# Folding the column frequencies of an inverse transform over plus and minus f, in a fused spectral and MLP block on one Trainium2 core

## The chip, the core and the metric

The kernel runs on one core of a Trainium2 chip. The metric is the device time of one execution in microseconds (us); the figure of a kernel is the median of its runs. For the kernel before the change, three runs gave 366.99, 367.8 and 368.43 us.

## The reference

Only what matters is kept: a layer norm with modulation, a two-dimensional spectral filter, a gated residual, and a Mish MLP with its own norm and gate. Sequence length is 2048, width 512, hidden width 1376, all float32.

```python
mod = (silu(c) @ w_mod).reshape(1, 6, 1, 512)
sa, ca, ga, sb, cb, gb = (mod[:, k] for k in range(6))
h = layernorm(x) * (1 + ca) + sa
x = x + ga * irfft2(rfft2(h) * (w_r + 1j * w_i), (2048, 512))
h = layernorm(x) * (1 + cb) + sb
x = x + gb * (mish(h @ w1 + b1) @ w2)
```

## The kernel before

The work has four stages, one behind the other, and TensorE runs through all of them. Every transform is a product with a constant matrix. A product of two float32 operands takes two passes over TensorE (so the trace counts two MATMUL records for it); the large MLP products are instead split by hand into a high and a low part in the type fp32r, and three one-pass products (`TERMS`) make one.

**Stage one** takes the 16 slices n of 128 rows through the row transform (`p1_row`, L269) and the first half of the column transform (`p1_col`, L314 to L316).

**Stage two** (`p2_*`, L441 to L698) handles the 64 row frequencies q in 17 groups, mostly of four. For each q TensorE turns a 128x128 block (`p2_in`, L539); one product with the matrix `kf` for the whole group ends the forward transform (`p2_mul`, L559); ScalarE (ACT), GpSimd (POOL) and VectorE (DVE) multiply by the complex filter (`p2_prod`, L590 to L593) and add the two products (`p2_add`, L599) into `slot(g)`, which lies in `a_sb`; then for each q one product of 128 column frequencies by 128 with the matrix `kv` starts the way back (`p2_out`, L608). `store_d` copies the result into `dd`, where it stands on 128 partitions, one for each column frequency, with three planes: real, imaginary, and minus real. The third plane is written by ACT (L454), DVE (L456) or POOL (L458). The group of q = 0 has its own path (`z_in` to `z_out`, with the helper `reflected`). The seven `mod_late` sums of modulation columns (L176 on DVE) are placed between the groups.

**Stage three** ends the column transform. For each n and each of four j, `p3_col` forms one sum of two products: real and imaginary planes times `kc[0]` (L859), imaginary and minus real planes times `kc[1]` (L860). ACT copies the result out of PSUM (`buf`, L862), `p3_row` does the row transform with the gated matrix `kiv` (L869), DVE adds to x (L872), and ACT takes the sums for the second norm (`row_squares`, L876 and L877). Beside it ACT and DVE split the weights w1 into high and low parts (L739, L740), form the sums of blocks of w1 (L760) and of w2 (`sum_w2`, L913, into `tsum`) that Strassen's scheme needs, split those too (L916, L917, L926, L1339), and bring the first rows of the normed x into the layout of the MLP (`norm_one`, L219; `turn_near`, L798; a round trip through memory; `scale_turned`, L825; `split_in`, L850 and L851).

**Stage four** is the MLP on eight blocks b of 256 rows, taken in four pairs i. The up products use Strassen's seven products (`up`, L991) but for the first pair, which is plain (`PLAIN`, L974). After Mish, `sums` (L1061) forms four block sums, `halves` splits the blocks (L916, L917), and `down` (L1091) does seven products for each hidden tile t, with three terms of 256 columns each: 21 passes. `gather`, `chain` and `residual` (L1114 to L1143) put the seven results together, multiply by the gate, and POOL's queue adds the block to x by a DMA.

Stages one and two are written out by hand in program order. Stages three and four are recorded as steps in a `Plan`, and the table of numbers `ORDER` sets the order in which the steps are issued. Within an engine the issued order is the executed order.

## Time and profile before

| What | Value |
|---|---|
| Median of the three runs | 367.8 us |
| Profiled execution, its own time | 368.36 us |
| Its span, first to last instruction | 366.6 us |
| Granted TensorE clock | 0.997 |
| TensorE busy in the span | 358.6 us (98%) |
| DVE busy | 302.5 us (83%) |
| ACT busy | 266.9 us (73%) |
| POOL busy | 78.3 us (21%) |

The profile shows one execution. "PE" rows are products on TensorE, "PEld" rows the loading of their stationary operand. Busy time of PE overstates its work, since the record of a product runs on while the next one already streams; so the pace of products is read here from start to start, not from the mean of a row. A line number is that of the kernel whose trace it is.

### The profile page before, as it was taken

Reading aid. Unit: us, or ns where it says so; the run is one execution under the profiler, and the core shown is the slowest. Engines: PE = TensorE matmul, PEld = TensorE weight load, DVE = VectorE, ACT = ScalarE, POOL = GpSimd, SP = SyncE. Lnnn points to the kernel's source line nnn. Section 1 sums busy time; section 2 is a strip of 40 time slices with the busy share of each in tenths; the row PEclk is TensorE's granted clock in tenths of the full one; section 3 lists DMA queues with packets and bytes.
Section 4 is the critical chain, followed back from the end, with each engine's and each line's share of the span. In section 5 each row is a group of like instructions: output and inputs, shape, how many; then the busy total and the mean of one; then the engine's idle time right before and its main releaser. Section 6 shows DMA issues by size and latency. Waiting matters only on the chain.

```text
span 366.6 us, 7820 instructions
## 1 busy us (share of the span) xinstructions
PE 358.6 (98%) x2666; PEld 333.9 (91%) x2666; DVE 302.5 (83%) x752; ACT 266.9 (73%) x601; POOL 78.3 (21%) x126
## 2 busy tenths in 40 slices
PE   8999999998999999999999999999999999999994
PEld 8999977777999998798999999999999999999994
DVE  1898968888889799998994777998759977887995
ACT  1798879996799999998773878766577753555650
POOL 0588738786011001100002101004100000000000
PEclk9999999999999999999999999999999999999998
DMA  7999997678498776899888877786989678863133
GB/s 254 383 349 377 331 373 250 219 185 305 142 327 254 236 256 230 278 306 322 248 225 292 276 236 200 207 276 206 281 301 243 215 229 266 227 219 62 59 57 115
DMA packets 54343, 89.96 MB, mean 245 GB/s; under 512 B 7552, under 2 KB 20960, under 8 KB 54048
## 3 DMA queue, kind: packets, MB, share of 16 engines
q1 hardware_dynamic: 49728, 74.65, 62.0%
q0 software_dynamic: 2416, 7.87, 9.0%
q10 hardware_dynamic: 2160, 6.95, 6.0%
q8 instruction: 21, 0.34, 0.4%
q14 instruction: 18, 0.15, 0.1%
HBM read 68.21 MB, written 17.57 MB: 234 GB/s over the span
## 4 chain that ended last, share of the span: by engine, by line
PE 84%; ACT 5%; DVE 4%; DMA 2%; POOL 1%; issue 1%; ACTq 1%; SPq 0%; DVEq 0%; POOLq 0%
PE bank L1091 25%; PE bank L991 22%; PE bank L974 6%; PE bank L269 4%; PE bank L869 4%; PE bank L859 3%; PE bank L860 3%; PE bank L1037 3%; PE bank L314 3%; PE bank L1087 3%; DMA hT<-in_B_w_dram 2%; PE bank L1103 2%; PE bank L316 1%; PE bank L315 1%; PE bank L325 1%
## 5 line engine op out<-in xcount | busy, mean ns | idle before, releaser
L991 PE MATMUL bank<-hT,wr 128*128 128x256 f32 x360 | 51.6, 283 | 0.0
L991 PEld LDWEIGHTS bank<-hT,wr 128*128 128x128 f32 x360 | 47.3, 191 | 0.6
L991 PE MATMUL bank<-hB,wr 128*128 128x256 f32 x318 | 46.6, 285 | 0.0
L991 PEld LDWEIGHTS bank<-hB,wr 128*128 128x128 f32 x318 | 41.9, 191 | 0.9
L1143 POOL DMA_DIRECT2D x<-modr x7 | 6.3, 898 | 140.5 <-DVE modr L1142 84.7
L1091 PE MATMUL bank<-w2a,ah 128*128 128x256 f32 x161 | 35.1, 283 | 0.0
L917 DVE TENSOR_TENSOR al<-buf,ah 128x512 fp32r<-128x512 f32 (+1 forms) x45 | 30.1, 668 | 5.7 <-ACT ah L916 4.7
L1091 PE MATMUL bank<-w2b,ah 128*128 128x256 f32 x147 | 32.2, 283 | 0.0
L916 ACT CAST ah<-buf 128x512 fp32r<-128x512 f32 (+1 forms) x45 | 27.0, 602 | 4.5 <-DVE buf L1061 2.6
L1091 PEld LDWEIGHTS bank<-w2a,ah 128*128 128x128 f32 x161 | 27.0, 191 | 0.4
L859 PE MATMUL bank<-kc,d 128*128 128x128 f32 x128 | 24.9, 276 | 0.5 <-ACT d L452 0.5
L1091 PEld LDWEIGHTS bank<-w2b,ah 128*128 128x128 f32 x147 | 24.9, 191 | 0.3
L860 PE MATMUL bank<-kc,d 128*128 128x128 f32 x128 | 24.8, 275 | 0.0
L974 PE MATMUL bank<-hB,wr 128*128 128x512 f32 x96 | 24.4, 393 | 0.0
L1091 PE MATMUL bank<-w,ah 128*128 128x256 f32 x112 | 21.5, 284 | 0.0
L314 PE MATMUL bank<-buf,mring 128*128 128x512 f32 x48 | 20.6, 430 | 0.2 <-DVE buf L307 0.2
L974 PEld LDWEIGHTS bank<-hB,wr 128*128 128x128 f32 x96 | 17.3, 189 | 3.1
L859 PEld LDWEIGHTS bank<-kc,d 128*128 128x128 f32 x128 | 19.4, 192 | 0.7 <-ACT d L452 0.7
L860 PEld LDWEIGHTS bank<-kc,d 128*128 128x128 f32 x128 | 19.5, 192 | 0.0
L1091 PEld LDWEIGHTS bank<-w,ah 128*128 128x128 f32 x112 | 17.7, 191 | 0.6
L608 PEld LDWEIGHTS bank<-kv,a_sb 128*128 128x128 f32 x126 | 15.5, 192 | 2.8 <-issue 2.2
L788 POOL DMA_DIRECT2D turned<-x x16 | 8.9, 568 | 42.1 <-DVE x L782 42.1
(310 smaller groups left out, 1098.2 us busy)
## 6 DMA issues: line engine op xcount, KB each, us to landing
wr<-w_S SPq DMA_DIRECT2D x60, 256.0 KB, 4.0
wr<-w_A SPq DMA_DIRECT2D x45, 256.0 KB, 3.8
w_S<-hT SPq DMA_DIRECT2D x20, 256.0 KB, 2.9
x<-in_A_x_dram SPq DMA_DIRECT2D x16, 256.0 KB, 4.7
xring<-in_x_t_dram SPq DMA_DIRECT2D x16, 256.0 KB, 4.6
w_A<-wr SPq DMA_DIRECT2D x15, 256.0 KB, 3.1
x<-modr POOLq DMA_DIRECT2D x7, 512.0 KB, 5.5
out_dram<-x SPq DMA_DIRECT2D x7, 512.0 KB, 3.8
```

Source lines behind the costliest of these rows:

```text
L269: nc.tensor.matmul(pgv[:, j], data(j), krs[:, j, :].rearrange("p (c q) -> p c q", c=2), start=True, stop=True)
L314: nc.tensor.matmul(pa, m[:, a, 0:128], g, start=(i == 0), stop=False)
L608: nc.tensor.matmul(pd[:, i * P:(i + 1) * P], y[:, i * P:(i + 1) * P], kv[:, 0:128], start=True, stop=True)
L859: nc.tensor.matmul(o, dj[:, 0:128], kc[0][:, n, :], start=True, stop=False)
L860: nc.tensor.matmul(o, dj[:, 64:192], kc[1][:, n, :], start=False, stop=True)
L869: nc.tensor.matmul(px[:, j * P:(j + 1) * P], e[:, j * P:(j + 1) * P], kiv[:, j, :], start=True, stop=True)
L916: nc.scalar.copy(h, r)
L917: nc.vector.tensor_tensor(l, r, plain(h), op=ALU.subtract)
L974: nc.tensor.matmul(ups[i, t, f], ring[t, a][:, p, b, :], sides[int(a[2]) - 1][:, :, q, b, :], start=(a[2] == "1" and b == 0 and n == 0), s ...
L991: nc.tensor.matmul(o, w[:, p, k, :], h[:, q, k, :], start=(first and n == 0), stop=(last and n == 5), skip_group_check=True)
L1037: nc.tensor.matmul(ups[i, 0][:FL], w1s[:, p, u, :], sides[u // 2][:, :, q, u % 2, :], start=(u == 0 and p + q == 0), stop=(u == 3 and p == ...
L1091: nc.tensor.matmul(out_ps[b][n][:, 256 * half:256 * half + 256], a[p][:, e], w2[t][q][:, r], start=(t == 1 and half == 0 and i == 0), stop ...
```

## The change

1. **Signs and fold.** The 128 column frequencies stand in a new order, 64, -1 to -63, 0 to 63, so that plus and minus f lie 64 columns apart. After the filter two new operations per group (`fold`) replace the two halves by their difference and their sum. The column matrix then needs cosines for one half and sines for the other, and `p3_col` needs one product where it had two. `kc` is half as large, and the third plane of `dd` is gone.
2. **The way back in halves.** The sums and the differences need different matrices (`kv` and i times `kv`), so each product of L608 becomes two, each with 64 columns of the stationary operand, into 64 partitions of the result (`half`). The column of frequency 64, which has no partner, needs a small product of its own for each batch of groups (`spin_mul`), and a copy back (`spin_copy`).
3. **First superblock plain through w2.** `PLAIN_DOWN = 2`: blocks b = 0 and 1 do `down` without Strassen, 12 passes of 512 columns for each t where there were 21 of 256; `sums`, `gather` and `chain` fall away for them, and `halves` splits 512 columns where it split 896.
4. **Sums of w2 later.** They are formed only behind block 1, from w2 loaded once more (`load_sums`, two loads for each t).
5. **Steps on GpSimd.** The first four `norm_one`, the first 16 operations of `scale_turned`, and the scaling in `row_squares` move from ACT to POOL.
6. **Order.** Stage two is recorded as a `Plan` as well, and both stages have new tables (`ORDERS`).

The core of the diff (constants and the q = 0 path are cut):

```diff
+PLAIN_DOWN = 2
-RAW = ((0, 0, 0, 0), (1, 0, 2, 1), (2, 0, 1, 6))
-SUM = ((0, 1, 3, 3), (3, 0, 4, 4), (3, 1, 5, 5), (1, 1, 6, 2))
+RAW = ((0, 0, 0, 0), (1, 0, 2, 1), (2, 0, 1, 5))
+SUM = ((0, 1, 3, 3), (3, 0, 4, 6), (3, 1, 5, 4), (1, 1, 6, 2))
...
-    dd = [big.tile([P, 8, 4, 3, NQ], F32, name=f"d{i}", tag=t) for i, t in enumerate(("da", "db"))]
+    dd = [big.tile([P, 8, 4, 2, NQ], F32, name=f"d{i}", tag=t) for i, t in enumerate(("da", "db"))]
...
-            if kind == "all":
-                nc.scalar.mul(minus, s[:, :, 0, :], -1.0)
-            elif kind != "pool" and i:
-                nc.vector.tensor_scalar(minus, s[:, :, 0, :], -1.0, None, op0=ALU.mult)
-            else:
-                nc.gpsimd.tensor_scalar(minus, dst[:, :, 0, q0:q0 + nq], -1.0, None, op0=ALU.mult)
...
+    def half(out, rows, *products):
+        o = out[rows:rows + 64]
+        for n, (a, b) in enumerate(products):
+            nc.tensor.matmul(o[0:1] if a.shape[1] == 1 else o, a, b, start=(n == 0), stop=(n == len(products) - 1))
...
+    def fold(g, step):
+        less, more = halves_of(g)
+        if step == 0:
+            on = nc.gpsimd if FOLD(g) else nc.vector
+            on.tensor_tensor(less, more, less, op=ALU.subtract)
+        else:
+            nc.vector.scalar_tensor_tensor(more, more, 2.0, less, op0=ALU.mult, op1=ALU.subtract)
...
+    def spin_mul(gs):
+        st["pd", gs[0]] = pd = bank("DA"[gs[0] > 14])
+        y = single(gs)
+        nc.tensor.matmul(pd[:, 0:y.shape[1]], kv[:, 6 * P:7 * P], y, start=True, stop=True)
+
+    def spin_copy(gs):
+        y = single(gs)
+        nc.scalar.copy(y, st["pd", gs[0]][:, 0:y.shape[1]])
...
-            nc.tensor.matmul(pd[:, i * P:(i + 1) * P], y[:, i * P:(i + 1) * P], kv[:, 0:128],
-                             start=True, stop=True)
+            for lo in (0, 64):
+                half(pd[:, i * P:(i + 1) * P], lo, (y[:, i * P + lo:i * P + lo + 64], kv[:, P - 2 * lo:2 * P - 2 * lo]))
...
+    BATCHES = [(1, 2), (3, 4), (5, 6), (7, 8), (9, 10), (11, 12), (13, 14), (15,), (16,)]
...
-        st["h2", n] = norm(n, True)
+        st["h2", n] = norm(n, n > 3)
...
-            nc.scalar.activation(o, o, AF.Identity, bias=cols[:, 1, 0, k:k + 1], scale=cols[:, 1, 1, k:k + 1])
+            if near:
+                nc.gpsimd.tensor_scalar(o, o, cols[:, 1, 1, k:k + 1], cols[:, 1, 0, k:k + 1], op0=ALU.mult, op1=ALU.add)
+            else:
+                nc.scalar.activation(o, o, AF.Identity, bias=cols[:, 1, 0, k:k + 1], scale=cols[:, 1, 1, k:k + 1])
...
-            nc.tensor.matmul(o, dj[:, 0:128], kc[0][:, n, :], start=True, stop=False)
-            nc.tensor.matmul(o, dj[:, 64:192], kc[1][:, n, :], start=False, stop=True)
+            nc.tensor.matmul(o, dj, kc[0][:, n, :], start=True, stop=True)
...
-        nc.scalar.mul(mv[:, n, 0:1], mv[:, n, 0:1], -D ** -1.5)
+        nc.gpsimd.tensor_scalar(mv[:, n, 0:1], mv[:, n, 0:1], -D ** -1.5, None, op0=ALU.mult)
...
+    def load_sums(t):
+        for e, f, rows in tiles(t):
+            nc.sync.dma_start(modr[:rows, e], w2_d[f * P:f * P + rows, :])
...
-        if b == NB - 1 and t > 2:
+        if b < PLAIN_DOWN or b == NB - 1 and t > 2:
             parts[b, t] = [(w, slice(0, 4))]
             return
...
+            if t and b < PLAIN_DOWN:
+                n, half, f = piece
+                w = w2[t][q]
+                w = w[:, 1:3] if f else w[:, 0:4:3]
+                nc.tensor.matmul(out_ps[b][n], a[p][:, half + 2 * f], w, start=(t == 1 and f == 0 and i == 0),
+                                 stop=(t == NT - 1 and f == 1 and i == 2), skip_group_check=True)
...
+    for t in range(1, NT):
+        at = start[PLAIN_DOWN - 1, t] + 3
+        plan.at(at, load_sums, t)
+        plan.at(at + 1, sum_w2, t, 0, 1, 2, 3)
+        plan.at(at + 2, split_w2, t, True)
```

How the order moves at three places. First TensorE at the end of stage two and the start of stage three, before. `kv,a_sb` is the way back, `wide,kf` and `buf,kf` the last forward products, `kc,d` the column products:

```order
L559 MATMUL bank<-wide,kf 128x512
L608 MATMUL bank<-kv,a_sb 128x128 x4
L559 MATMUL bank<-buf,kf 128x512
L608 MATMUL bank<-kv,a_sb 128x128 x20
L859 MATMUL bank<-kc_1088,d_749 128x128
L860 MATMUL bank<-kc_1116,d_749 128x128
```

The same place of the changed kernel, where `a_sb,kv` is `spin_mul` and `64x128` are the halves:

```order
L566 MATMUL bank<-buf,kf 128x512
L480 MATMUL bank<-kv,a_sb 64x128 x16
L633 MATMUL bank<-a_sb,kv 128x4
L633 MATMUL bank<-a_sb,kv 128x8
L480 MATMUL bank<-kv,a_sb 64x128 x24
L633 MATMUL bank<-a_sb,kv 128x4
L480 MATMUL bank<-kv,a_sb 64x128 x8
L974 MATMUL bank<-kc,d_749 128x128 x8
L983 MATMUL bank<-kiv,buf 128x128 x4
```

The way back now comes in batches of two groups, twice as many products of half the height, with small products between; the column products alternate no longer between two matrices.

Second DVE in the middle of stage two, before. L593 is the filter product, L599 the addition, L456 and L450 the third plane and the copy into `dd`:

```order
L599 TENSOR_TENSOR a_sb<-bank,wide 128x512
L593 TENSOR_TENSOR bank<-bank,wqa 128x512
L456 TENSOR_SCALAR d_750<-bank 128x32x4
L599 TENSOR_TENSOR a_sb<-bank,buf 128x512
L593 TENSOR_TENSOR bank<-bank,wqa 128x512
L450 COPY d_750<-bank 128x32x2x4
L456 TENSOR_SCALAR d_750<-bank 128x32x4
```

And of the changed kernel (L622 and L624 are the two steps of `fold`):

```order
L622 TENSOR_TENSOR a_sb<-a_sb 128x4x63
L612 TENSOR_TENSOR a_sb<-bank,buf 128x512
L624 SCALAR_TENSOR_TENSOR a_sb<-a_sb 128x4x63 x2
L622 TENSOR_TENSOR a_sb<-a_sb 128x4x63
L456 COPY d_750<-bank 128x64x4
L608 TENSOR_TENSOR bank<-bank,wqa 128x512
L624 SCALAR_TENSOR_TENSOR a_sb<-a_sb 128x4x63 x2
L612 TENSOR_TENSOR a_sb<-bank,buf 128x512
```

The operation for the third plane is gone, and up to two fold operations per group stand between addition and filter product.

Third ACT at the start of stage three, before (`mv<-mv` is the scaling, `w_1221<-modr` the high part of the sums of w2):

```order
L862 COPY buf<-bank 128x512
L739 CAST hT_1311<-hT_1310 128x256
L739 CAST wr<-hT_1279 128x256
L916 CAST w_1221<-modr 128x1024
L876 ACTIVATE mv<-mv 128x1
L877 ACTIVATE bank,mv<-x,mv 128x512
L188 ACTIVATE rstd<-mv,eps 128x2
```

And of the changed kernel:

```order
L976 COPY buf<-bank 128x512
L196 ACTIVATE rstd<-mv,eps 128x2
L197 ACTIVATE rstd<-rstd 128x2
L991 ACTIVATE bank,mv<-x,mv 128x512
L976 COPY buf<-bank 128x512 x2
L851 CAST hT_1413<-hT_1412 128x256
```

The scaling and the sums of w2 have left the queue, and the splits of w1 come later.

422 lines of the change are left out of this document (241 added, 181 removed), and 97 rows, old and new, of tables (ORDER, ORDERS).

## The prediction

> **What bounds the kernel now.** I read the first part of the page, then the shares of the chain that ended last, then the busy time by stage. A window row gives its bounds, its length, and then busy us and instructions of PE, PEld, DVE, ACT and POOL, the granted clock, and the DMA share and rate.
>
> ```profile
> PE 358.6 (98%) x2666; PEld 333.9 (91%) x2666; DVE 302.5 (83%) x752; ACT 266.9 (73%) x601; POOL 78.3 (21%) x126
> ...
> PE 84%; ACT 5%; DVE 4%; DMA 2%; POOL 1%; issue 1%; ACTq 1%; SPq 0%; DVEq 0%; POOLq 0%
> ```
>
> ```profile
> 49.60:90.00 40.40, 38.86 (x240) 28.42 (x239) 33.92 (x73) 36.33 (x88) 30.15 (x52) 1.00 0.78 265
> 90.00:129.10 39.10, 38.74 (x343) 38.55 (x344) 33.85 (x95) 35.58 (x91) 2.86 (x5) 1.00 0.75 238
> 129.10:146.30 17.20, 17.20 (x122) 15.96 (x121) 16.24 (x46) 16.39 (x43) 1.07 (x2) 1.00 0.73 242
> 146.30:177.30 31.00, 31.00 (x185) 27.21 (x184) 28.73 (x73) 28.67 (x68) 1.09 (x2) 1.00 0.92 301
> 177.30:220.00 42.70, 42.70 (x345) 41.88 (x344) 32.87 (x87) 29.11 (x59) 5.34 (x9) 1.00 0.84 250
> ```
>
> TensorE is the bound in every stage, at full clock: 84% of the chain lies on it. So the change is worth what it takes from TensorE's queue, as long as the others keep up. In stage two (first row) and stage three (the next two) ACT and DVE are at 84% to 95% themselves, so a shorter TensorE queue meets them soon; after 177.3 they have room. POOL has room from 90 on.
>
> The pace of products comes from the timeline, start to start (start, length, engine, line):
>
> ```profile
> 118.52 1.06 PE L869 MATMUL bank<-kiv,buf 128*128 128x128 f32 x8
> 119.41 0.39 PE L859 MATMUL bank<-kc,d 128*128 128x128 f32 x2
> 119.63 0.39 PE L860 MATMUL bank<-kc,d 128*128 128x128 f32 x2
> ```
>
> ```profile
> 65.59 1.02 PE L559 MATMUL bank<-buf,kf 128*128 128x512 f32 x2
> 66.45 0.60 PE L539 MATMUL bank<-ident,a_sb 128*128 128x128 f32 x4
> 66.89 0.39 PE L475 MATMUL bank<-kv,early 128*128 128x128 f32 x2
> 67.20 0.38 PE L476 MATMUL bank<-kv,early 128*1 128x128 f32 x2
> 67.51 0.49 PE L478 MATMUL bank<-kw,early 96*128 96x128 f32 x2
> ```
>
> Four products (eight passes) of L869 take 0.89 us, one of L859 0.22 us: a 128x128 product of two passes costs 0.223 us. A product with `kf` takes 0.86 us, four turns 0.44. L476 uses one column of the stationary operand and streams 128: it takes 0.31 us like the full L475 ahead of it. Each is about 0.09 us over the pace, which I read as the price of a change of shape; without it the one-column product costs as much as a full one.
>
> **The change, part by part.** All is summed against the profiled execution (368.36 us, span 366.6); it lies 0.56 us above the median of 367.8, to which I carry the sum.
>
> *Column products.* These rows give the counts in passes (two for one product):
>
> ```profile
> L859 PE MATMUL bank<-kc,d 128*128 128x128 f32 x128 | 24.9, 276 | 0.5 <-ACT d L452 0.5
> L860 PE MATMUL bank<-kc,d 128*128 128x128 f32 x128 | 24.8, 275 | 0.0
> L608 PE MATMUL bank<-kv,a_sb 128*128 128x128 f32 x126 | 16.7, 278 | 0.9 <-DVE a_sb L599 0.7 <-ACT d L454 0.2
> ```
>
> One of the two lines goes: 64 products at 0.223 us, **-14.3 us** of TensorE. Before, stage three is TensorE's from end to end, so nothing else hides this time.
>
> *The way back in halves.* 63 products of L608 cost 14.0 us; 126 halves replace them. Their price is in no row. From above, a half streams the same 128 columns as L476, so 0.223 us each, 28.1 in all. From below, half the work of a full product, 0.112 us each, 14.0 in all. The one-column row would speak for the upper end, but there a single product stands between two full ones; here the halves alternate between two sets of 64 columns and two sets of 64 result partitions in runs of 14 to 24, and one needs nothing of the other. I take the lower end as the likelier: the two share one product's time, and TensorE's sum stays as it was. The upper end is the first rival.
>
> The Trainium skill, page "TensorEngine Tiling (Array Packing)", section "Tiling Modes", says that tiles of 128x64 work independently and can run in parallel, and that a change of mode drains the engine. By it the halves would cost 14 us and not 28; the 0.09 us around L476 agrees with the drain, and no run here shows two halves side by side.
>
> Added to TensorE are nine small products (at 0.223 us, bound by the one-column row, 2.0 us), about 18 changes of shape around nine runs of halves (at 0.09, 1.6 us), and some 0.4 us in the q = 0 path: +4.0 us. TensorE's work in stage two is now 16 products with `kf` (13.8), 63 turns (6.9), 14.0 and about 2 for q = 0, 36.7 of 40.4 us; it becomes 40.7.
>
> *DVE in stage two.*
>
> ```profile
> L456 DVE TENSOR_SCALAR d<-bank 128x128 f32<-128x128 f32 x9 | 2.6, 284 | 0.5 <-ACT d L452 0.5
> L913 DVE TENSOR_TENSOR modr<-wide 128x256 f32<-128x256 f32 x10 | 4.2, 415 | 0.0
> L176 DVE SCALAR_TENSOR_TENSOR wm<-wm,bank 128x512 f32<-128x512 f32 x7 | 4.7, 679 | 0.0
> ```
>
> The third plane goes (-2.6 us), two of the seven modulation sums move ahead of the stage (-1.4). Of the 32 fold operations 25 stand on DVE, each 252 elements a partition; by the nearest row, 256 elements in 0.415 us, +10.4 us. 33.9 becomes 40.3 us in a stage of 40.4. It was 6.5 us idle, mostly while the first groups fill the pipeline, and it will not work without gaps; the additions behind the folds wait in the same queue, and TensorE waits for those. Bounds: nothing if the folds overlap perfectly, +6.5 if all the old idle time stays. I take **+5.0 us** for the stage, in which TensorE's own +4.0 lies hidden. ACT there loses L454 and gains nine small copies,
>
> ```profile
> L454 ACT ACTIVATE d<-bank 128x128 f32<-128x128 f32 x7 | 2.1, 295 | 0.0
> L521 ACT COPY early<-bank 32x1 f32<-32x1 f32 x1 | 0.1, 150 | 0.0
> ```
>
> about equal. POOL loses 13 planes at 0.53 and gains seven folds,
>
> ```profile
> L458 POOL TENSOR_SCALAR d<-d 128x128 f32<-128x128 f32 x13 | 6.8, 530 | 0.0
> L262 POOL TENSOR_TENSOR mring<-mraw,mring 128x256 fp32r<-128x256 f32 x16 | 12.2, 763 | 13.2 <-ACT mring L261 13.2
> ```
>
> -6.9 and +5.3 in 30.2 us. Neither binds.
>
> *Plain down for two blocks.* From the chain, in runs:
>
> ```profile
> 146.46 6.14 PE bank L974 x27
> 176.84 1.44 PE bank L1091 x12
> ```
>
> 512 columns in fp32r take 0.227 us, 256 take 0.120. Per block and t, 12 x 0.227 = 2.73 against 21 x 0.120 = 2.52; ten of them, **+2.1 us** of TensorE, with nothing to hide it. What it takes from DVE and ACT (four sums, the smaller split, `gather` and `chain`) lies beside TensorE.
>
> *Steps on POOL, later sums.*
>
> ```profile
> L876 ACT ACTIVATE mv<-mv 128x1 f32<-128x1 f32 x16 | 3.2, 200 | 0.0
> L219 ACT ACTIVATE buf<-x,nmr,rstd 128x512 f32<-128x512 f32 x8 | 6.3, 818 | 0.0
> L825 ACT ACTIVATE wide<-wide,cols 128x256 f32<-128x256 f32 x12 | 6.5, 593 | 0.0
> L916 ACT CAST w2a<-modr 128x1024 fp32r<-128x1024 f32 x1 | 1.0, 1042 | 0.0
> L917 DVE TENSOR_TENSOR w2a<-modr,w2a 128x1024 fp32r<-128x1024 f32 x1 | 1.2, 1217 | 0.0
> ```
>
> Between 90 and 129.1 ACT loses about 14 x 0.2, 4 x 0.82, 8 x 0.59 and two casts of sums at 1.04: about 13 of 35.6 us, as much as TensorE loses (14 of 16 slices, 12.5), so its share stays near 85%. DVE loses eight sums at 0.415 and two splits at 1.217, 5.8 of 33.9: 28.1 us remain, where TensorE needs 39.1 - 12.5 = 26.6. So DVE becomes the longer by **+1.5 us**; from 129.1 on it has twelve sums and three splits less and catches up, so this is not paid twice. POOL takes these 36 operations, none over the 0.82 us that ACT needs for the longest if POOL is no slower, where it was busy for 4 of 56 us; at twice ACT's price they are some 32 us and still fit. What is queued behind them is its sends of normed rows, and the split of the first blocks waits for those. The later sums (5 x (4 x 0.415 + 1.22) = 14.4 us of DVE) fall where 177.3 to 220 shows DVE at 77%, and blocks 0 and 1 give back about as much. Ten more loads of 256 KB there, 2.6 MB beside 10.7 MB (42.7 us at 250 GB/s), feed sums that block 2 is the first to need, so other blocks' products hide them; if a load came late, its transfer of about 1 us at that rate and the sum and split behind it would stand open, some 4 us once. One load of `kc` falls away.
>
> Sum: -14.3 + 5.0 + 2.1 + 1.5 = **-5.7 us**, so 362.7 by the profiled execution and **362.1 us** by the median.
>
> **The rivals.**
>
> *The halves do not overlap* (slower). Each costs 0.223 us, TensorE in stage two gets 40.7 + 14.0 = 54.7 us, and DVE's 40.3 hide under it. With 2 us of gaps the stage takes 56.7, +16.3: -14.3 + 16.3 + 2.1 + 1.5 = +5.6, **373.4 us**. For it speaks L476, against it that the halves are disjoint. It decides from about 0.19 us a half, where the stage takes as much as the column products give back.
>
> *They overlap in part*, 0.15 to 0.18 us a half: 5 to 8 us more on TensorE, of which DVE's slack hides little: **367 us**.
>
> *ACT and DVE keep stage three.* Then half of the 14.3 us arrives, and the rest is a wait of the row products for L862 and L872: **368 us**. For it speaks that both are over 85% busy there; against it, that the sums show them relieved by about as much.
>
> **How the numbers follow.** About 0.5% is what a measurement of this kernel can tell from no change: 366.0 to 369.6 us counts as the same. Forecast case 0.58 (357 to 366.5), full price of the halves 0.26 (369 to 377), part price 0.11 (364 to 370), stage three held 0.05 (366 to 370). Faster: nearly all of the first and half of the third, 0.61. Same: 0.13. Slower: most of the second, 0.26. The range reaches from 357 (DVE costs nothing in stage two) to 373.5 (most of the second case) and leaves out about 0.17.
>
> **What would show it.** In the changed trace: the start-to-start pace of the halves (L480), 0.11 us for the forecast and 0.22 for the first rival; DVE nearly without gaps from the first filter product to the last fold (L622, L624), and a stage two of about 45 us; four column products (L974) in 0.89 us with the row products (L983) right behind; 0.227 us for a pass of the plain down (L1206). The prediction is wrong if TensorE stands still in stage three for lack of L976 or L986, or if stage two is over 50 us long.

## The result and the profile after

The changed kernel takes 372.55 us, the median of four runs (371.27 to 373.39), against 367.9 us of the kernel before: 1.0126 times its time, 95% interval 1.0086 to 1.0166. So it is slower by 4.7 us, where 362.1 us was forecast. The profiled execution took 373.39 us, its span is 371.6 us, 5.0 more than before.

First the same two lines of the page: busy times, and the shares of the chain that ended last.

```profile
PE 355.2 (96%) x2598; PEld 319.3 (86%) x2598; DVE 296.7 (80%) x708; ACT 248.3 (67%) x549; POOL 98.5 (27%) x156
...
PE 58%; DMA 14%; DVE 12%; ACT 4%; issue 4%; POOL 3%; SPq 3%; ACTq 0%; DVEq 0%; POOLq 0%
```

TensorE has less work than before (358.6 us were busy) and holds only 58% of the chain, where it held 84%. The time went to waits, of transfers and of DVE above all. The windows by stage tell where (bounds, length, busy us and instructions of PE, PEld, DVE, ACT and POOL, granted clock, DMA share and rate):

```profile
49.60:62.00 12.40, 8.85 (x42) 5.32 (x41) 6.71 (x15) 6.79 (x15) 4.55 (x10) 0.86 0.74 285
62.00:102.38 40.38, 36.47 (x353) 25.29 (x351) 37.46 (x77) 29.28 (x75) 25.31 (x37) 1.00 0.54 170
102.38:141.30 38.92, 37.78 (x314) 36.47 (x315) 31.96 (x91) 32.65 (x82) 16.83 (x31) 1.00 0.76 243
141.30:180.00 38.70, 38.70 (x175) 31.74 (x175) 28.58 (x68) 28.50 (x69) 8.63 (x13) 1.00 0.96 319
180.00:230.00 50.00, 47.42 (x312) 42.05 (x311) 39.45 (x85) 36.45 (x69) 5.37 (x9) 1.00 0.92 307
```

Stage two starts at 49.8 us as before, but the first column product stands at 102.4 us and not at 90.0: the stage takes 52.6 us where it took 40.4, so 12.2 us more. What follows takes 269.2 us where it took 276.6, 7.4 us less. Two rows stand out: the first 12.4 us of stage two, with TensorE busy for 71% (8.85 of 12.40 us), the others for under 60%, and a granted clock of 0.86, and 180 to 230 us, where TensorE had not waited at all before.

**The start of stage two.** The timeline there (start, length, engine, line, and in brackets the idle time ahead of it with what ended it):

```profile
51.60 0.69 DVE L184 SCALAR_TENSOR_TENSOR wm<-wm,bank 128x512 f32<-128x512 f32 x1 [3.15 <-DMA wm<-in_w_mod_dram]
...
52.22 0.68 DVE L184 SCALAR_TENSOR_TENSOR wm<-wm,bank 128x512 f32<-128x512 f32 x1
...
53.14 0.37 DVE L357 TENSOR_REDUCE saz<-modr 128x16 f32<-128x128 f32 x1
...
53.66 0.51 POOL L558 TENSOR_TENSOR early<-early,saz 128x3 f32<-128x3 f32 x3 [7.05 <-DVE saz L357]
...
53.91 3.22 PE L566 MATMUL bank<-early,kf 128*128 128x384 f32 x4 [2.40 <-POOL early L558]
```

Read it from the bottom: the first product with `kf` (L566) waits for POOL's shift, the shift for DVE's `saz` (L357), and this stands in DVE's queue behind two modulation sums (L184) that wait until 51.5 us for their weights `wm`. These two were among the groups before; the new table puts them at DVE's head. After the 2.4 us without a product the granted clock is 0.54 for 3.2 us:

```profile
53.90:57.10 3.20, 3.19 (x6) 1.53 (x7) 0.88 (x2) 0.96 (x2) 0.73 (x3) 0.54 1.04 406
```

**From 180 to 230 us.** The chain there (start, length, what):

```profile
202.88 6.55 DMA modr<-in_B_w_dram
...
213.30 0.83 PE bank L1105 x5
214.13 4.54 DMA wr<-w_S
218.81 0.95 PE bank L1105 x6
```

The transfers `modr<-in_B_w_dram` are the new loads for the later sums of w2 (L1024), and `wr<-w_S` are the fetches of w1, of which one was issued at 214.13, right behind a load that had waited for its buffer. I count TensorE's loss from start to start: the distance of each product to the next, less the median distance of its kind, added up. From 180 to 240 us it is 4.5 us (0.3 before); it is given for some of the runs below in the same way.

**What came as forecast.** Halves and column products:

```profile
86.54 1.97 PE L480 MATMUL bank<-kv,a_sb 128*64 128x128 f32 x32
...
105.27 1.06 PE L974 MATMUL bank<-kc,d 128*128 128x128 f32 x8
106.16 1.06 PE L983 MATMUL bank<-kiv,buf 128*128 128x128 f32 x8
107.05 1.06 PE L974 MATMUL bank<-kc,d 128*128 128x128 f32 x8
```

Sixteen halves (32 passes) take 1.9 us, 0.12 us each, so two of them share the time of one product. Four column products take 0.89 us (105.27 to 106.16), and row products follow them without a gap. So the first rival's mechanism did not happen, though its time (373.4 us) is near the measured one.

One execution each of e10 and e12 below was in a slower state of the chip, and their medians leave it out.

### The profile page after: what moved, and what is told of

Its sections match the earlier page's. It is cut to its first block, busy times and chain, and to the rows that moved or that the text cites. A ratio compares the mean times of both kernels' runs of the same rounds, so it can differ in the third digit from the quotient of the medians.

```text
span 371.6 us, 7670 instructions
## 1 busy us (share of the span) xinstructions
PE 355.2 (96%) x2598; PEld 319.3 (86%) x2598; DVE 296.7 (80%) x708; ACT 248.3 (67%) x549; POOL 98.5 (27%) x156
## 4 chain that ended last, share of the span: by engine, by line
PE 58%; DMA 14%; DVE 12%; ACT 4%; issue 4%; POOL 3%; SPq 3%; ACTq 0%; DVEq 0%; POOLq 0%
PE bank L1105 17%; PE bank L1214 17%; PE bank L1088 6%; PE bank L1206 4%; DMA modr<-in_B_w_dram 3%; DMA wm<-in_w_mod_dram 3%; PE bank L1151 3%; PE bank L1210 2%; DMA wqa<-in_w_q_dram 2%; PE bank L974 2%; PE bank L277 1%; PE bank L983 1%; DMA xring<-in_x_t_dram 1%; DMA x<-modr 1%; PE bank L333 1%
## 5 line engine op out<-in xcount | busy, mean ns | idle before, releaser
L1105 PE MATMUL bank<-hT,wr 128*128 128x256 f32 x360 | 51.5, 284 | 1.1 <-DMA wr<-w_S 1.1
L1214 PE MATMUL bank<-w2a,ah 128*128 128x256 f32 x119 | 25.9, 283 | 0.0
L1214 PE MATMUL bank<-w2b,ah 128*128 128x256 f32 x105 | 23.1, 283 | 0.0
L1214 PEld LDWEIGHTS bank<-w2a,ah 128*128 128x128 f32 x119 | 19.8, 191 | 0.1
L1214 PEld LDWEIGHTS bank<-w2b,ah 128*128 128x128 f32 x105 | 17.9, 191 | 0.6
L480 PEld LDWEIGHTS bank<-kv,a_sb 128*64 128x64 f32 x252 | 13.6, 137 | 5.3 <-ACT d L458 2.4
L983 PE MATMUL bank<-kiv,buf 128*128 128x128 f32 x128 | 17.0, 278 | 0.6 <-DVE x L986 0.5
L974 PE MATMUL bank<-kc,d 128*128 128x128 f32 x128 | 16.7, 276 | 0.5 <-ACT d L458 0.5
L277 PE MATMUL bank<-modr,xring 128*128 128x128 f32 x128 | 16.7, 275 | 0.0
L1033 DVE TENSOR_TENSOR al<-even,ah 128x384 fp32r<-128x384 f32 (+1 forms) x15 | 8.7, 580 | 9.9 <-ACT ah L1032 9.9
L480 PE MATMUL bank<-kv,a_sb 128*64 128x128 f32 x252 | 15.7, 276 | 1.0 <-ACT a_sb L637 1.0
```

Of the source, the lines that this page charges most:

```text
L277: nc.tensor.matmul(pgv[:, j], data(j), krs[:, j, :].rearrange("p (c q) -> p c q", c=2), start=True, stop=True)
L480: nc.tensor.matmul(o[0:1] if a.shape[1] == 1 else o, a, b, start=(n == 0), stop=(n == len(products) - 1))
L974: nc.tensor.matmul(o, dj, kc[0][:, n, :], start=True, stop=True)
L983: nc.tensor.matmul(px[:, j * P:(j + 1) * P], e[:, j * P:(j + 1) * P], kiv[:, j, :], start=True, stop=True)
L1033: nc.vector.tensor_tensor(l, r, plain(h), op=ALU.subtract)
L1105: nc.tensor.matmul(o, w[:, p, k, :], h[:, q, k, :], start=(first and n == 0), stop=(last and n == 5), skip_group_check=True)
```

## Experiments

All eighteen runs, each beside the kernel before on the same chip. "Stage two" is the time from the first turn to the first column product, "loss" TensorE's loss from 180 to 240 us; both are of the run's profile, and a blank means that it is not given.

| Run | Edit | Median us | Ratio to before, 95% interval | Stage two | Loss |
|---|---|---|---|---|---|
| (changed kernel) | | 372.55 | 1.0126, 1.0086 to 1.0166 | 52.6 | 4.5 |
| e1 | early sums moved back | 369.57 | 1.0054, 1.0034 to 1.0073 | 48.5 | 4.8 |
| e2 | loads on GpSimd's queue | 380.69 | 1.0355, 1.0322 to 1.0388 | 52.8 | 12.6 |
| e3 | e1 and e2 | 378.28 | 1.0292, 1.0263 to 1.0321 | | |
| e4 | halves in rows | 374.79 | 1.0187, 1.0144 to 1.0229 | 55.9 | |
| e5 | e1, rounds of sums earlier | 376.88 | 1.0244, 1.0214 to 1.0274 | | 5.3 |
| e6 | e1, 14 folds on GpSimd | 371.73 | 1.0093, 1.0068 to 1.0117 | 49.1 | |
| e7 | e1, no folds | 367.94 | 0.9997, 0.9976 to 1.0018 | 46.3 | 6.8 |
| e8 | e1, all folds on DVE | 372.36 | 1.0118, 1.0101 to 1.0135 | 51.1 | |
| e9 | e1, second buffer for the sums | 379.15 | 1.0303, 1.0279 to 1.0326 | | 13.4 |
| e10 | e1, no small products | 369.98 | 1.0061, 1.0032 to 1.0090 | 47.8 | |
| e11 | e1, more banks | 370.47 | 1.0060, 1.0036 to 1.0084 | 49.6 | |
| e12 | e9 and e11 | 379.25 | 1.0316, 1.0274 to 1.0357 | 48.5 | |
| e13 | e1, no loads | 366.09 | 0.9944, 0.9925 to 0.9962 | 48.5 | 0.7 |
| e14 | e1, pieces rebuilt on GpSimd | 373.03 | 1.0141, 1.0118 to 1.0163 | | 7.3 |
| e15 | e7 and e10 | 364.97 | 0.9925, 0.9908 to 0.9943 | 43.5 | |
| e16 | e1, loads moved in the queue | 372.97 | 1.0138, 1.0111 to 1.0166 | | 7.6 |
| e17 | e1, scaling back on ACT | 375.76 | 1.0213, 1.0190 to 1.0236 | | |
| e18 | e1, pieces rebuilt on DVE | 370.30 | 1.0069, 1.0042 to 1.0097 | | 4.3 |

### The two stalls

**e1.** Steps 61 and 98 of the table are the two sums; they move behind the filter products of groups 1 and 2.

```diff
-    "5-9 4 10-14 24 15 19 16 22 35 17 59 61 98 0 20 18 28-30 21 36 23 25 40 37 41 52 83 47 55 31 53 32 39 48 38 26 "
+    "5-9 4 10-14 24 15 19 16 22 35 17 59 0 20 18 61 28-30 21 36 23 25 40 37 41 52 83 47 55 31 98 53 32 39 48 38 26 "
```

> The changed kernel, with its first two modulation sums (L184) moved in the table of stage two: no longer DVE's first steps, but behind the filter products (own) of the first and the second group. Their loads stay where they are in SyncE's queue. Theory (DVE stood 3.2 us at the head of the stage until the loads of wm landed at 51.5 us, and the reductions that give saz, the shifts and the first product with kf stood behind it): the gap of 2.7 us ahead of the first L566 goes, the granted clock of 0.54 from 53.9 to 57.1 us goes with it, DVE's first L608 starts near 53 instead of 58.2 us, and the kernel takes 4 to 5 us less, about 368. Rival (the stage is DVE's anyway, and DVE only meets its work later): the first L608 comes earlier, but the last L974 starts no more than 1.5 us earlier, and the time is 371 or more.

Measured 369.57 us, 3.0 less. In its timeline and window the gap and the low clock are gone:

```profile
51.32 1.67 PE L566 MATMUL bank<-early,kf 128*128 128x384 f32 x4
```

```profile
49.60:62.00 12.40, 11.24 (x61) 7.12 (x61) 10.37 (x24) 10.01 (x21) 8.29 (x19) 1.00 0.86 309
```

The four passes take 1.67 us where they took 3.22. The time fell short of the 4 to 5 us that the theory gave; stage two is 4.1 us shorter in the profile. The last column product (L974) starts 4.1 us earlier, so the rival falls. All later runs but e2 and e4 stand on e1.

**e2 and e3.** The loads leave SyncE's queue, alone and on top of e1.

```diff
-            nc.sync.dma_start(modr[:rows, e], w2_d[f * P:f * P + rows, :])
+            nc.gpsimd.dma_start(modr[:rows, e], w2_d[f * P:f * P + rows, :])
```

> The changed kernel, with the ten loads of w2 for the later sums (L1024) issued from GpSimd's queue instead of SyncE's. Theory (a load waits in SyncE's queue until its buffer modr is read out, and the fetches of w1 behind it are issued too late, so that L1105 waits for them between 190 and 220 us): TensorE loses under 1 us instead of 4.6 us between 180 and 220, and the kernel takes 3 to 4 us less, about 369. Rival (the 2.6 MB more are too much for the transfers there, which run at 400 GB/s from 198 to 206 us): the fetches are issued earlier but land as late, TensorE still loses 4 us there, and the time stays at 372 to 373. A second rival is that the sends of normed rows, now behind the loads in GpSimd's queue, come late, and block 2 or 3 waits for its rows: then the time is the same or worse.

> Both edits at once: the two early modulation sums behind the first groups' filter products, and the loads for the sums of w2 on GpSimd's queue. If both theories hold and the two stalls are independent, the savings add: 7 to 9 us under the changed kernel, 363.5 to 365.5 us, and so 2 to 4 us faster than the kernel before. If stage two is bound by DVE whatever its start, or the transfers bind at 200 us, 368 us or more.

Both were wrong: 8.1 us slower than the changed kernel, and 378.28 us together. The waits of DVE in e2 (180 to 240 us: who waits for whom, us in total, times, longest):

```profile
DVE modr L1029 <- DMA modr<-in_B_w_dram: 10.2, 8, 2.3
```

and those of TensorE (185 to 240 us):

```profile
PE bank L1105 <- DVE odd L1134: 2.9, 2, 2.4
PE bank L1105 <- issue: 1.8, 1, 1.8
PE bank L1105 <- DVE buf L1134: 1.5, 1, 1.5
```

SyncE's fetches are free now, but the loads come later, DVE stands at the head of the sums (L1029) for 10.2 us, and TensorE waits for DVE's work behind them (L1134). So SyncE's queue was not the whole cause. Part of the time is the clock: ahead of its end e2's trace has three stretches of 3.4 us at half the clock (from 55.4, 195.4 and 236.3 us), of which the changed kernel has only the one in stage two (from 53.5 us); e3 has one (from 190.2 us). The second of e2:

```profile
195.40:198.80 3.40, 3.40 (x13) 3.11 (x14) 2.44 (x3) 2.33 (x6) 1.58 (x3) 0.50 0.33 86
```

Each can cost TensorE up to half its length, 1.7 us. The five rounds (load, four sums, cast, subtraction, and only then the next load into the same buffer) are one chain.

**e5.** Three of the five rounds move ahead of block 0's residual, by the table alone (the steps of rounds 1 to 3 behind the steps at places 233 to 325, those of rounds 4 and 5 to where 1 and 2 stood). The sums overwrite one of the four pieces of w2 that the plain products of blocks 0 and 1 still read, so here these read other values, and the splits have to wait for products of block 0.

> As e1 (early modulation sums behind the first groups), and the sums of w2 earlier in the table of the later stages: three of the five rounds (two loads, four sums on DVE, a split on ACT and DVE) ahead of block 0's residual, two behind it, where all five stood behind it. The queue of the loads stays SyncE's. Theory, new after e2: the five rounds are one chain through one buffer (load about 5 us, sums 1.8, cast 1.1, subtraction 1.2, some 9 us a round), 45 us from block 0's residual on, while block 2 wants all five by about 215 us; DVE and ACT, which run in order, stand waiting in them, and TensorE loses 4.8 us between 180 and 230 us in e1. With three rounds ahead, TensorE should lose under 1 us there: 4 us under e1, 365 to 366 us, faster than the kernel before. Rival (the transfers bind): the loads now add to a stage whose DMA share is 0.95 already (140 to 180 us), TensorE loses 2 us or more there or between 180 and 230, and the time is 368 or more.

Measured 376.88 us. It was a bad experiment: a loss came in ahead, where TensorE is busy for 34.6 of the 40 us from 140 to 180 (40.0 in e1), and that from 180 to 240 us stayed (5.3 us). The reason why the sums stand so late is in the code: with the whole computation they cannot begin before block 1 has used the piece.

**e9 and e12.** Rounds 2 and 4 get the tile `wide("y")`, and each load is issued a round ahead (e12: with the banks of e11).

```diff
+    def sum_space(t):
+        return modr[:, 0:2] if t % 2 else wide("y")
...
-            nc.sync.dma_start(modr[:rows, e], w2_d[f * P:f * P + rows, :])
+            nc.sync.dma_start(sum_space(t)[:rows, e], w2_d[f * P:f * P + rows, :])
```

> As e1, with a second buffer for the later sums of w2: rounds 2 and 4 load into the tile that holds the next block's rows, which is free then, and each load is issued a round ahead. The five splits stay behind block 1's products, which read one of the four pieces that they overwrite. Theory (five rounds through one buffer are one chain of some 9 us each, and in-order engines wait in it): loads overlap the sums and splits of the round before, DVE no longer waits for the loads, and TensorE loses under 2 us between 180 and 230 us instead of 4.8: 366 to 367.5 us. Rival (transfers bind, at 400 GB/s in places): the loads come earlier and land later, the fetches of w1 are late as before, TensorE still loses 4 us there: 369 to 370 us.

> e9 and e11 together: early sums behind the first groups, a second buffer for the sums of w2, more banks for the way back. If both theories hold, the savings add: 365 to 366.5 us, 1.5 to 3 us under the kernel before. If neither does, 369.5 us.

379.15 and 379.25 us, far worse than either theory. A load that is issued a round ahead waits longer at the head of SyncE's queue, since the second tile comes free at 191.5 us only, and the fetches of w1 wait behind it (waits of TensorE, 165 to 250 us):

```profile
PE bank L1111 <- DMA wr<-w_A: 4.5, 2, 2.5
...
PE bank L1111 <- DMA wr<-w_S: 2.3, 2, 1.8
```

Here too the clock adds to it: it was at 0.50 to 0.51 for 3.4 us from 197.8, from 208.1 and from 232.0 us in e9, and from 206.7 us in e12.

**e13.** The loads are left out, all else stays.

```diff
-            nc.sync.dma_start(modr[:rows, e], w2_d[f * P:f * P + rows, :])
+            pass
```

> As e1, with the ten loads for the later sums of w2 left out (the sums are then formed of what the buffer holds, so the values are other ones; sums, casts and subtractions are all there). It prices the loads. Theory (the loads hold SyncE's queue until the buffer is free, the fetches of w1 behind them come late, and DVE and ACT wait for the loads at the head of their queues): TensorE loses under 1.5 us between 180 and 230 us instead of 4.8, and the time falls by 3 to 4.5 us, to 365 to 366.5. Rival (DVE's and ACT's work for the sums itself is what is late there): TensorE still loses 3 us or more there, 368.5 to 369.5 us.

366.09 us, and the loss falls from 4.8 to 0.7 us. The window:

```profile
180.00:230.00 50.00, 49.86 (x351) 46.10 (x350) 43.42 (x93) 38.87 (x74) 5.34 (x9) 1.00 0.89 274
```

So the ten loads, with the waits that they bring, cost 3.5 us, nearly all that is lost there; DVE's and ACT's work for the sums fits (43.4 of 50 us).

**e16.** Only round 2 has the second tile, and the loads stand behind more fetches (rounds 2 and 3), the sums later (round 2) or earlier (rounds 4 and 5).

```diff
+    def sum_space(t):
+        return wide("y") if t == 2 else modr[:, 0:2]
```

> As e1, with a second buffer for round 2 alone (the tile of the block's rows, free from about 191 us on), and the steps of the five rounds moved so that SyncE reaches a load when its buffer has come free, and DVE reaches the sums when the load has landed: the loads of rounds 2 and 3 behind three and four more fetches of w1, the sums of round 2 some 4 us later, the sums of rounds 4 and 5 and their loads some 1 to 2 us earlier. Theory (e13: what costs is engines and queues that stand at the head of a round, not the 2.6 MB): TensorE loses under 2 us between 180 and 230 us instead of 4.8, 366.5 to 368 us. Rival (the transfers themselves, beside the fetches of w1, make both late whatever the order): TensorE loses 4 us or more as in e1 and e9, 369.5 us or more.

372.97 us, loss 7.6: the rival's number. But the trace does not speak for transfers as such: TensorE waited 2.3 us for ACT's copy behind the cast of a round, 1.8 and 1.1 us for fetches, and SyncE's queue stood from 203.9 to 209.5 and from 213.5 to 218.1 us ahead of the loads of rounds 4 and 5. The order did not take the waits away.

**e14 and e18.** No loads: the pieces are added up from their high and low parts, which lie in the chip's memory, on GpSimd (e14) or on DVE (e18).

```diff
-        for e, f, rows in tiles(t):
-            nc.sync.dma_start(modr[:rows, e], w2_d[f * P:f * P + rows, :])
+        hi, lo = (plain(w) for w in w2[t])
+        for e, k in enumerate((slice(0, 4, 3), slice(1, 3))):
+            nc.gpsimd.tensor_tensor(tsum[:, 2 * e:2 * e + 2], hi[:, k], lo[:, k], op=ALU.add)
```

> As e1, with no loads for the later sums: GpSimd adds the high and the low part of each piece of w2, which lie in the chip's memory already, into the buffer (two additions of 128x512 a round, near 1.3 us each by L604), and the rest of a round is as it was. Theory (as in e13, the loads are what costs, by SyncE's queue and by the length of a round): a round takes 6.6 us and not 9, SyncE's queue never waits for the buffer, TensorE loses under 2 us between 180 and 230 us, 365.5 to 367 us, faster than the kernel before. Rival (GpSimd's additions slow DVE, since both work on the same memory, or the sends behind them come late): 368 or more.

> As e14 (no loads; the pieces of w2 put together again from high and low part), but DVE does the ten additions instead of GpSimd, 0.6 to 0.7 us each: 6 to 7 us more for DVE, which is busy for 39 of 50 us between 180 and 230 in e1. Theory (in e14 a DVE operation of 0.28 us takes 1.3 us whenever one of GpSimd's additions runs, and that is where e14 loses): without GpSimd at work the rounds are 5.5 us long, nothing waits for a transfer, TensorE loses under 2 us between 180 and 230 instead of 7.3, and the time is 366 to 367.5 us. Rival (DVE has no room for 6 us more there, whoever shares the memory): TensorE loses 4 us or more, 369.5 to 372 us.

e14 takes 373.03 us, its rival's side, and its timeline shows why:

```profile
199.47 2.58 POOL L1025 TENSOR_TENSOR modr<-w2hi,w2a 128x512 f32<-128x512 f32 x2 [3.61 <-DVE w2a L1034]
199.63 1.28 DVE L1176 TENSOR_TENSOR buf<-even 128x128 f32<-128x128 f32 x1
200.95 1.27 DVE L1176 TENSOR_TENSOR buf<-buf,even 128x128 f32<-128x128 f32 x1
202.14 0.28 DVE L1176 TENSOR_TENSOR buf<-even 128x128 f32<-128x128 f32 x1
202.34 0.28 DVE L1176 TENSOR_TENSOR buf<-even,buf 128x128 f32<-128x128 f32 x1
```

Four equal operations of DVE: the two that meet GpSimd's two additions take 1.28 us, as long as an addition of GpSimd, the two behind them 0.28. In e18, without GpSimd's additions, the same operations stay at 0.28, the loss falls from 7.3 to 4.3 us and the time to 370.30, the rival's range. So the sharing costs e14 about 3 us; the rest of its loss stays, and DVE has little room for the work:

```profile
180.00:230.00 50.00, 48.06 (x326) 42.88 (x325) 45.14 (x95) 36.59 (x70) 5.35 (x9) 1.00 0.81 261
```

DVE is busy for 45.1 of 50 us, and TensorE loses nearly as much as with the loads (4.8 us in e1).

### What else lengthens stage two

**e4.** In the changed kernel, without e1:

```diff
-        for i in range(nq):
-            for lo in (0, 64):
+        for lo in (0, 64):
+            for i in range(nq):
```

> The changed kernel with the halves of the way back in another order: for a group first all products into the lower 64 partitions, then all into the upper 64, instead of in turns. The work is the same. Theory (two halves side by side share the time of one product, since they use different columns and partitions): products that follow each other on the same columns can't overlap, a half then takes 0.22 us instead of 0.11, TensorE gets some 13 us more in stage two, of which its waits for DVE hide a part (it is idle or slowed for about 12 of 52.6 us there): 377 to 384 us. Rival (the pace of 0.11 us belongs to a half as such, with 64 columns of the stationary operand): the pace stays at 0.11 us and the time at 372.5.

374.79 us, 2.2 more: neither the theory's time nor the rival's. Sixteen halves now take

```profile
91.69 2.57 PE L480 MATMUL bank<-kv,a_sb 128*64 128x128 f32 x32
94.19 0.39 PE L633 MATMUL bank<-a_sb,kv 128*128 128x8 f32 x2
```

2.5 us, 0.156 us each: between the two prices. The first five passes of this run stand 0.11 us apart, as for products that can't overlap; in the middle they overlap, with passes that start ahead of their place. The trace shows it by the pass that signals the end of the first group: it is the sixteenth in the queue, and starts as the nineteenth (in the changed kernel as the sixteenth). So the order matters, and the pace of 0.12 us is not a half's own; but TensorE mends part of a bad order itself.

**e6, e7 and e8.** Folds on GpSimd, none, all on DVE:

```diff
-        return g % 2 and g < 15
+        return g < 15
```

> As e1, with the first fold step of 14 groups on GpSimd instead of seven. Theory (DVE sets the pace of stage two: 43.7 us busy of 48.7): it loses seven operations of 0.33 to 0.6 us, GpSimd gets 7 of 0.75, stage two shortens by 2 to 4 us: 366 to 368 us. Rival (folds on DVE are slow because GpSimd works on the same memory at that time, and additions wait for GpSimd's products): DVE's second steps get longer, GpSimd's products come later, and the time stays at 369.5 or rises.

> As e1, with all 32 fold operations left out (the way back then gets the unfolded spectrum, so the values are other ones, the work of every other step the same). It prices the folds on the path. Theory (DVE is the bound of stage two): DVE loses 13 us of 43.7, TensorE's own work of some 39 us is next, and stage two shrinks from 48.5 to 43 or 44 us: 364.5 to 366 us. Rival (the stage is longer for the small products between the batches, which wait for the copies out of the result banks, and for the filling of its pipeline): it shrinks by under 2 us, and the time is 368 or more.

> As e1, with all 32 fold operations on DVE, so that GpSimd has seven fewer. Theory (DVE is the bound): seven more at 0.35 to 0.6 us, 2.5 to 4 us on the path: 372 to 373.5 us. Rival (GpSimd's share of the memory is what makes the folds long, and with less of it the others get shorter): the 25 other folds lose up to 2 us, and the time rises by under 1.5 us, 371 or less.

(e8 has `return False` there, e7 a `return` at the head of `fold`.) More folds on either engine made it slower: 371.73 and 372.36 us against 369.57, so the split of the changed kernel is the best of the three; e6's theory was wrong, and e8 took the time that its theory gave. Without any fold the stage is 2.2 us shorter, not 4.5 to 5.5: DVE is not its only bound. The time fell by 1.6 us to 367.94, close to the rival's 368; e7's profile loses 6.8 us from 180 to 240 us, with a clock of 0.51 for 3.4 us from 207.2 us, so the gain of the stage is in part lost again.

**e10, e11 and e15.** No small products, more banks, neither folds nor small products:

```diff
-                st["pd", g] = bank("DA"[g > 14])
+                st["pd", g] = bank("DA"[g > 14 or g in (8, 10, 12)])
```

(e11; e10 has a `return` at the head of `spin_mul` and of `spin_copy`, e15 all three.)

> As e1, with the nine small products (spin_mul) and the nine small copies behind them left out: the column of frequency 64 then goes unturned into the way back, all other work is the same. It prices the added small work of stage two. Theory (what TensorE itself got is on the path beside DVE's folds, since the two wait for each other in turns): their 2.2 us on TensorE and most of the 2.9 us of waits around them go, stage two gets 3 to 4.5 us shorter than 48.5, 365 to 366.5 us. Rival (DVE is the bound, and TensorE's own additions lie under it, as the prediction had it): under 1 us shorter, 369 us.

> As e1, with the results of the way back of groups 8, 10 and 12 in the two banks that the turned blocks used, so that a batch of two groups no longer needs both banks that the batch before it still holds. Theory (the small product that opens a batch waits until ACT and DVE have copied the batch before out of its banks): the waits ahead of the small products, 1.5 us in e1, shrink to under 0.5, and the time falls by 0.5 to 1.5 us, to 368 to 369. Rival (the batches wait for DVE's additions and folds anyway): no change, 369.6 us.

> As e1, with the folds and the small products with their copies left out both (other values, the rest of the work the same). e7 took 2.2 us from stage two (48.5 to 46.3), e10 0.8 (to 47.8). Theory (TensorE's small products and DVE's folds cover each other in part, so that each alone hides behind the other): both together give more than the sum, 4 us or more, a stage of 44.5 us or less. Rival (they are independent waits): the sum, 3 us, 45.5 us.

e11 changed nothing within its interval: the waits moved from the small products to the halves behind them. Its stage of 49.6 us is 1.2 us longer than e12's, though the two have the same stage two, so a difference of about 1 us between two profiles need not be the edit's. e10 took 0.8 us from the stage and nothing from the time, its rival's side. But e15 took 5.0 us from the stage (48.5 to 43.5) and 4.6 from the time, where e7 and e10 add up to 3.0. The windows of the whole stage, of e1, then e15:

```profile
49.76:98.30 48.54, 43.42 (x390) 29.78 (x388) 43.74 (x91) 35.99 (x88) 29.76 (x46) 1.00 0.61 203
```

```profile
49.84:93.37 43.53, 40.89 (x373) 27.57 (x371) 32.77 (x65) 35.17 (x79) 24.35 (x39) 1.00 0.69 227
```

TensorE and DVE are each busy for some 43.5 of 48.5 us in e1, and each stands for about 5 us; by the records only 0.3 us of that are common to both. So neither alone sets the length. What the halves wait for is in the code and in the waits: behind the addition (`p2_add`) there are two branches, the folds, and the small product with ACT's copy of its result (L637), and the halves need both. TensorE's waits ahead of the halves, in e1 and then in e10, which has no small products:

```profile
PE bank L480 <- ACT a_sb L637: 1.0, 2, 0.7
```

```profile
PE bank L480 <- DVE a_sb L622: 1.2, 1, 1.2
```

In e1 the copy comes last; without it the halves wait for a fold instead. Take one branch away, and the other still holds them. These waits of 1 us or so are not all of the 5.0 us; how the rest comes about is not shown.

**e17.** The first 16 operations of `scale_turned` go back to ACT.

```diff
-            if near:
+            if False:
```

> As e1, with the first 16 operations of scale_turned back on ACT, as in the kernel before. In e1 four of them stand in the chain (4.6 us on GpSimd from 126 us on, ahead of the first product of the MLP). Theory (on GpSimd they take twice ACT's 0.59 us and set the start of the MLP's first products): TensorE's waits between 120 and 140 us, 1.3 us in e1, fall by half or more, and the time by 0.5 to 1 us, to 369. Rival (ACT is as full there, and they wait in its queue): no change or up to 1 us more, 369.5 to 370.5 us.

375.76 us, 6.2 more: worse than the rival allowed. From 98.3 to 140 us ACT is busy for 37.4 us instead of 35.6, TensorE for 38.5 instead of 40.7, and it waits for ACT's splits of the rows:

```profile
PE bank L1105 <- ACT hB L965: 2.4, 2, 1.7
```

Behind the longest of these waits the granted clock is halved:

```profile
131.35 5.79 PE L1105 MATMUL bank<-hB,wr 128*128 128x256 f32 x24 [1.73 <-ACT hB L965]
```

```profile
130.60:137.40 6.80, 6.05 (x26) 5.73 (x27) 6.07 (x15) 6.63 (x18) 0.91 (x2) 0.50 0.75 246
```

This can be up to 3.4 us of the 6.2. The steps on GpSimd are a gain, though four of them stand in the chain.

No run that does the whole computation beats the kernel before; e1 is the best of the changed family, and e13 and e15, which do, leave work out.

## Why the prediction was wrong

The forecast lies 10.4 us under the measured median. That time lies below the upper end of the forecast's range (373.5 us) only because the range made room for the first rival, which did not happen. Point by point:

1. **Column products, -14.3 us: right.** Sixty-four products went, and four of the rest take 0.89 us.
2. **Halves at 0.112 us: right.** Measured 0.12 us, two side by side; e4 shows that it hangs on the order. The rule quoted from the Trainium skill, page "TensorEngine Tiling (Array Packing)", section "Tiling Modes", that such tiles run in parallel, is borne out by these 0.12 us. (The turning point of 0.19 us a half, given with the first rival, is 0.21 by the prediction's own sums: there the stage, with 2 us of gaps, is 14.3 us longer.)
3. **"Two of the seven modulation sums move ahead of the stage (-1.4)": wrong, 3.0 us.** I took the move from the order and counted the work, not the wait: the sums stand at DVE's head, their weights land at 51.5 us, and the reductions that start the stage are queued behind. The row of the sums shows nothing of that, their transfers' landing would have. Nor did their 1.4 us leave the stage: all seven sums run between 51.6 and 101.5 us, inside it. e1 gives back 3.0 us in the time and 4.1 in the stage, the low clock included.
4. **"I take +5.0 us for the stage, in which TensorE's own +4.0 lies hidden": wrong, 3.2 us.** Without the stall the stage takes 48.5 us, 8.2 more than before and not 5.0. The size of TensorE's term was near: its busy time in the stage grew from 38.86 us (the prediction's first window) to 43.42 (e1's), +4.6. But it does not lie hidden under DVE's: e7 and e10 give back 2.2 and 0.8 us, both together 5.0 (e15), since the halves wait for what both add. The maximum of two sums was the wrong model here. That is not the whole: without folds and small products the stage still takes 43.5 us, 3.2 more than before, and no run takes that apart. From start to start, the turns take 9.7 us of it (7.7 before) and the products with `kf` 14.1 (13.1 before). DVE's term was short as well: 43.7 us busy in e1 where 40.3 was forecast. The folds' rows of the changed kernel:

```profile
L624 DVE SCALAR_TENSOR_TENSOR a_sb<-a_sb 128x252 f32<-128x252 f32 (+1 forms) x16 | 7.7, 512 | 0.1
L622 DVE TENSOR_TENSOR a_sb<-a_sb 128x252 f32<-128x252 f32 x9 | 5.6, 627 | 0.0
```

   They are 13.3 us, where 25 times 0.415 gave 10.4. In e1 one of them takes 0.41 us alone (at 79.04) and 1.03 us beside an addition of GpSimd (at 83.45):

```profile
79.04 0.41 DVE L622 TENSOR_TENSOR a_sb<-a_sb 128x252 f32<-128x252 f32 x1
...
82.93 1.28 POOL L604 TENSOR_TENSOR buf<-buf,wqb 128x512 f32<-128x512 f32 x1
83.45 1.03 DVE L622 TENSOR_TENSOR a_sb<-a_sb 128x252 f32<-128x252 f32 x1
```

   My row for 0.415 came from a place where GpSimd did nothing.
5. **Plain down, +2.1 us: right in its price.** Twenty-one passes take 4.78 us in the chain, 0.228 us each:

```profile
173.50 4.78 PE bank L1206 x21
```

6. **"Ten more loads ... other blocks' products hide them": wrong, 3.5 us** (e13 against e1). The text allowed "some 4 us once"; it came in pieces, round by round. I priced bytes and asked when the sums are needed, and did not ask who stands behind a load that waits for its buffer: SyncE's fetches of w1, and DVE and ACT in the sums. Which of these costs how much is not settled. e2, e9 and e16 relieved one queue each, and the wait came back in another, larger each time, and in e2 and e9 a lower clock came with it.
7. **Steps on GpSimd, hidden: right**, and worth more than priced (e17, the lower clock there included).
8. **"DVE becomes the longer by +1.5 us" in stage three: right in size.** From the first column product to 180 us TensorE loses 2.3 us in e1 and 0.8 before. That DVE is the reason is not shown: of TensorE's three waits there in e1, of 0.5 us each, one is for DVE and two are for ACT. With the loads left out (e13), what follows stage two takes 265.7 us where it took 276.6, 10.9 less; the terms of points 1, 5 and 8 give 10.7.

The three wrong steps are 3.0 + 3.2 + 3.5 = 9.7 of the 10.4 us. This sum is rough: the first and the last are differences of medians from different chips (e1's interval alone is 0.7 us to either side), the second is a length in single profiles (where the stall of point 3 is 4.1 us). The rest, 0.7 us, is not assigned. Of what would make the prediction wrong, the stage two of over 50 us was named; the first rival, at nearly the measured time, was wrong in its mechanism, so the time alone would have taught the wrong lesson.

## What to carry to other kernels

When a table moves an operation to the head of an engine's queue, look up when its input lands, and who stands behind it; the same for a load into a buffer that is still in use, with the queue that issues it. Where a product waits for what two engines add, the larger addition does not hide the smaller: add the terms, or try both removed at once, before you take the larger one. And take the price of a VectorE operation from a row where GpSimd does what it will do at the new place.

## What the runs showed of the hardware

- In e14, DVE operations whose operands both lie in the chip's memory took 1.28 and 1.27 us while additions of 128x512 ran on GpSimd, and 0.28 us alone. The filter product L608, with one operand in a result bank, never took more than 0.70 us in e1, also beside such an addition (0.68 us at 82.85). The Trainium skill, page "SBUF — State Buffer", section "🔬 SBUF: two separate sides", says that the port pair the two share is an exclusive lock, held for a whole instruction; the 1.28 us, the length of GpSimd's own operation, agree with it.
- TensorE without a product for 2.4 us (51.5 to 53.9 us) ran at a granted clock of 0.54 for the next 3.2 us, with DMA at 406 GB/s; four passes took 3.22 us instead of 1.67. The length of the standstill alone does not decide it: behind 2.57 us in e5 (165.8 to 168.4 us) the clock stayed at 1.00, behind 1.08 us in e7 (206.1 to 207.1 us) it was 0.51 for 3.4 us.
- Halves on the same 64 columns, in rows, took 0.156 us each, where 0.22 was expected (e4): passes started ahead of their place, so that the sixteenth of a batch started as the nineteenth.
